# Transposes on two row tiles, PSUM as four fixed pairs, and a new order of the slot in a fused RWKV-7 and SoLU kernel

## The chip, the cores and the metric

The kernel runs on one core of one Trainium2 chip. A core has TensorE (matmuls, and the loads of their weights), VectorE, ScalarE and GpSimd for elementwise work, and SyncE, which here only issues DMAs. Every engine works through a queue of its own in order. Matmuls write PSUM, eight banks of 128 partitions by 512 float32; VectorE and ScalarE read it, GpSimd does not. The metric is the device time of one execution in microseconds.

## What is computed

Two blocks follow each other. The first is a recurrence over 768 tokens for 4 batches x 8 heads, each with a 40 x 40 state; the second takes its output, rearranged to 3072 tokens x 320, through a feed-forward layer with a softmax-weighted hidden layer and a normalisation.

```python
for t in range(S):                                   # batch 4, heads 8, S 768, D 40
    y[:, :, t] = einsum('bhd,bhde->bhe', rt, state)
    Sa = einsum('bhde,bhe->bhd', state, at)
    state = state * wt[:, :, None, :] - einsum('bhd,bhe->bhde', Sa, bt) + einsum('bhd,bhe->bhde', vt, kt)
x = y.transpose(0, 2, 1, 3).reshape(B * S, H * D)    # 3072 x 320
h = x @ w_in                                         # 3072 x 1024
solu = h * softmax(h)
ln = (solu - mean(solu)) / sqrt(var(solu) + 1e-6) * g_ln
out = ln @ w_out                                     # 3072 x 320
```

The weights of the second block are float64 and come in as their bits.

## The kernel before

**Tiling.** The recurrence is cut into chunks of 64 tokens. Two batches are stacked in the 128 partitions, so that there are N = 24 units of work (12 chunks x 2 pairs of batches), numbered `i`. Inside a unit the recurrence becomes small matrix products per batch and head, of 64 x 64, 64 x 40 or 40 x 64. TensorE runs them in its 64x64 form: four tiles of the array, two in the rows and two in the columns, each with its own weights. The products that use all 128 partitions (h, po, pcum) use the whole array.

**Stages of a unit.** `decay` takes logarithms of w, sums them with a matmul (pcum) and exponentiates. `decay_turned`, `front`, `front_b`, `attend_kv`, `attend_r` and `stated` transpose data from token rows to feature rows: `turned` (L347) makes four TensorE transposes of 128 partitions x 104 columns into one bank, and ScalarE or VectorE copies the result out. `norm` (L394) multiplies two of them, masks the product (`masked`, on VectorE) and writes it to DRAM, from where `spread` gathers 32 x 32 blocks for two units at a time. `invert` (L423) inverts these on VectorE in thirty steps of two instructions (prod, uu); the result goes through DRAM to `bring`. `flip`, `couple` and `close` complete the 64 x 64 inverse (tu); `scores`, `carried`, `driven`, `solved`, `answered`, `read` and `leave` compute the output of the unit and its new state.

**The feed-forward stages** run one to three units later, on the 128 tokens of a unit. `hidden` makes h (128 x 1024, two banks) from three slices of x: two of 128 rows, and one of 64 rows (`kt` = 2) whose two halves sit on the two row tiles. `highest`, `exped`, `weighed` and `spreadof` take the maximum (VectorE), the exponential with its sum (ScalarE), the product (VectorE), and the mean and variance by `bn_stats` (VectorE), with the power -1/2 on GpSimd. `folded` transposes the product in eight pieces of 128 x 128 (plnT), `output` multiplies by w_out in eight matmuls (po), and ScalarE scales the result on the way out (osb).

**PSUM** is held in three pools: `banks`, two buffers of two banks for everything on 64x64 tiles; h, one buffer of two banks; and `bank`, two single banks in turn for transposes, pcum, plnT and po. A buffer is taken by whoever asks next in the program, and its first matmul waits until the reader of the previous user is done.

**Order.** The order on every engine is written out by hand, in the loop at L823: each turn, or step, works on `i` (recurrence), `i + 1` and `i + 2` (its inputs), `j = i + 5` (the front of a later unit) and `m - 1` to `m - 3` with m = i - 1 (feed-forward). The inversion is dealt out in small numbers of steps between the other VectorE work (`some`, `narrow`; the tuple `pieces`). The first five steps also convert the weights to float32.

```python
L833        solved(i)
L837            scores(i + 1)
L844            stated(i); front(j)
L846        hidden(m - 2, ((0, 1),)); front_b(j); decay_turned(j + 1); hidden(m - 2, ((1, 1),))
L865        decay(j + 2); output(m - 3, 0)
L871        couple(i + 1); norm(j); answered(i); output(m - 3, 1)
L883        close(i + 1); read(i, True); carried(i + 1); hidden(m - 1, ((2, 0), (2, 1)))
L891        read(i, False); driven(i + 1); leave(i); folded(m - 2)
L896        hidden(m - 1, ((0, 0),)); attend_kv(i + 2); hidden(m - 1, ((1, 0),)); attend_r(i + 2)
```

Of the kernel before, what the change touches and what calls it, by code (L numbers as in the profile page):

```python
# [17 lines left out]
P = 128  # L18
# [9 lines left out]
THIN = (5, 15)  # L28
# [23 lines left out]
def kernel(  # L52
# [34 lines left out]
    ps1 = ctx.enter_context(tc.tile_pool(name="ps1", bufs=2, space=PSUM))  # L87
    ps2 = ctx.enter_context(tc.tile_pool(name="ps2", bufs=1, space=PSUM))
    ps3 = ctx.enter_context(tc.tile_pool(name="ps3", bufs=2, space=PSUM))
# [15 lines left out]
    nc.vector.memset(mhalf, -0.5)  # L105
    top = const.tile([P, 2], FP32, name="top")
# [15 lines left out]
    for x in ex_t:  # L122
# [10 lines left out]
                          in_=c_("eye_hi").unsqueeze(1).to_broadcast([P, 8, Q]))  # L133
    w_in = const.tile([P, 2 * NK - 1, DFF // 2], FP32, name="w_in")
# [4 lines left out]
    def banks(name):  # L139
        return ps1.tile([P, 2, 512], FP32, tag="banks", name=name)  # L140

    def bank(name):
        return ps3.tile([P, 512], FP32, tag="bank", name=name)
# [76 lines left out]
    def turn_g():  # L220
        pg = bank("pg")
        nc.tensor.transpose(out=pg[:, 0:NF], in_=g_rows, identity=ident[0:NF, 0:NF])
        for x, y in zip(g_cols, (0, -20, -36)):
            nc.scalar.mul(out=x, in_=pg[:, 0:NF], mul=2.0 ** y)
# [6 lines left out]
    def mean_of(lo, hi, begun):  # L231
        t = bank("pmean")
        nc.tensor.matmul(t[:, 0:DM], lhsT=ident, rhs=begun, start=True, stop=False)
        mean_part(t, lo, hi, False)
        return mean_kept(t)
# [90 lines left out]
    def decay(i):  # L326
# [5 lines left out]
        t = (bank("pcum") if i > 5 else ps2.tile([P, DFF], FP32, tag="h", name="h"))[:, 0:DM]  # L332
# [14 lines left out]
    def turned(name, x):  # L347
        t = bank("p" + name)
        for j in range(4):
            nc.tensor.transpose(out=t[0:W2, j * P:(j + 1) * P],  # L350
                                in_=x[:, 2 * j:2 * j + 2].rearrange("p a b -> p (a b)")[:, 0:W2], identity=ident)
        return t[0:W2].rearrange("p (j b t) -> p b j t", j=4, b=2)
# [9 lines left out]
    def decay_turned(i):  # L362
        if not ok(i):
            return
        ex = st[i]["ex"] = ex_t[i % (AHEAD + 2)]
        nc.scalar.copy(out=ex[0:W2, :, :, 1:], in_=turned("ei", ei_t[0]))

    def front(i):
        if not ok(i):
            return  # L370
        d = st[i]
        t = turned("a", d["raw_a"])
        aT = d["aT"] = tokens("aT", AHEAD)
        nc.vector.tensor_tensor(out=aT[0:W2], in0=t, in1=d["ex"][0:W2, :, :, 0:C], op=ALU.mult)

    def front_b(i):
        if not ok(i):
            return
        d = st[i]
        d["bT"] = kept("bT", turned("b", d["kb"][:, H:]))  # L380
# [13 lines left out]
    def norm(i):  # L394
# [3 lines left out]
        t = banks("pnt")  # L398
# [5 lines left out]
        masked(nt, t[:, :, 0:256])  # L404
# [18 lines left out]
    def invert(n):  # L423
# [6 lines left out]
        nc.vector.tensor_scalar(out=u[0:C], in0=nb[0:C, 0::2], scalar1=-1.0, scalar2=None, op0=ALU.mult)  # L430
# [36 lines left out]
    def couple(i):  # L467
# [3 lines left out]
        t = banks("py")  # L471
# [8 lines left out]
    def close(i):  # L480
# [3 lines left out]
        t = banks("pz")  # L484
# [8 lines left out]
    def attend_kv(i):  # L493
# [3 lines left out]
        d["kT"] = kept("kT", turned("k", d["kb"]))  # L497
        d["vT"] = kept("vT", turned("v", v_t[0]))

    def attend_r(i):  # L500
        if not ok(i):
            return
        st[i]["rT"] = kept("rT", turned("r", r_t[0]), 2)

    def stated(i):
        if not ok(i):
            return
        d = st[i]
        bp, ci = where_(i)
        if ci:  # L510
            t = bank("pst")
            for x in range(4):
                nc.tensor.transpose(out=t[0:W2, x * P:(x + 1) * P],  # L513
                                    in_=st_t[bp][:, 2 * x:2 * x + 2].rearrange("p a b -> p (a b)")[:, 0:W2], identity=ident)
            d["s"] = two.tile([P, 4, P], FP32, tag="s", name="s", bufs=1)
            nc.scalar.copy(out=d["s"][0:W2], in_=t[0:W2].rearrange("p (x t) -> p x t", x=4))

    def scores(i):
# [3 lines left out]
        t = banks("ps")  # L522
# [13 lines left out]
    def carried(i):  # L536
# [5 lines left out]
        d["px"] = banks("px")  # L542
# [21 lines left out]
    def solved(i):  # L564
# [3 lines left out]
        t = banks("pu")  # L568
# [14 lines left out]
    def answered(i):  # L583
# [3 lines left out]
        t = banks("pl")  # L587
# [6 lines left out]
    def read(i, own):  # L594
# [4 lines left out]
        if own:  # L599
            d["po"] = banks("pyo")  # L600
# [8 lines left out]
        for g in range(2):  # L609
            for j in range(2):  # L610
# [50 lines left out]
    def hidden(i, some):  # L661
# [4 lines left out]
        for kt, x in some:  # L666
            if (kt, x) == (NK - 1, 0):
                d["h"] = ps2.tile([P, DFF], FP32, tag="h", name="h")
            part = slice(0, P) if kt < 2 else half(x)
            mm(d["h"][:, 512 * x:512 * x + 512], d["xT"][part, kt], w_in[part, 2 * kt + (x if kt < 2 else 0)],  # L670
               start=kt == NK - 1, stop=kt == NK - 2)
# [16 lines left out]
    def weighed(i):  # L688
        if not ok(i):
            return  # L690
        d = st[i]
        nc.vector.tensor_tensor(out=d["e"], in0=d["h"], in1=d["e"], op=ALU.mult)  # L692

    def spreadof(i):
        if not ok(i):
            return
        d = st[i]
        bs = small.tile([P, 2, 6], FP32, tag="bs", name="bs")
        for x in range(2):
            nc.vector.bn_stats(out=bs[:, x], in_=d["e"][:, x * 512:x * 512 + 512])  # L700
        mv = small.tile([P, 2], FP32, tag="mv", name="mv")
        nc.vector.bn_aggr(out=mv, in_=bs)
        c = small.tile([P, 1], FP32, tag="c", name="c")
        c2 = small.tile([P, 1], FP32, tag="c2", name="c2")
        rs = d["rs"] = small.tile([P, 1], FP32, tag="rs", name="rs")
        nc.vector.tensor_scalar(out=c, in0=d["esum"], scalar1=1e-9, scalar2=None, op0=ALU.add)
        nc.vector.scalar_tensor_tensor(out=c2, in0=c, scalar=1e-6, in1=c, op0=ALU.mult, op1=ALU.mult)
# [224 lines left out]
```

## Time and profile before

| | |
|---|---|
| timed runs | 618.14, 618.70, 620.32 us (median 618.7) |
| the profiled execution, first to last instruction (span) | 616.2 us |
| TensorE, matmuls / weight loads | busy 552.0 us (90%) / 401.9 us (65%) |
| VectorE, ScalarE, GpSimd | busy 449.0, 265.8, 258.0 us (73%, 43%, 42%) |
| first pu of unit 4 / of unit 19 / of unit 23 | 161.4 / 485.3 / 561.7 us |
| mean clock granted to TensorE | 0.93; 0.52 to 0.64 from 19 to 115 us, 1.00 from 137 to 562 us |

The page gives no other time of its own for the profiled execution than its span. In its lines, PE is a matmul, PEld a weight load, DVE VectorE, ACT ScalarE and POOL GpSimd. A row of the windows gives the stretch, its length, then for each engine its busy time and its instructions, the granted clock, and the DMA engines' share and rate. A row of the timeline gives start, duration from the first start to the last end, engine, line, operation, the tile names, rows x columns of the stationary operand, partitions x columns of the output, and how many instructions; matmuls overlap, so the time that one group takes from the next is read from start to start. A float32 matmul is two instructions, a transpose one.

### The profile page before, as it was taken

What the parts mean: (1) busy time and instruction counts of PE and PEld (TensorE: products, weight loads), DVE (VectorE), ACT (ScalarE), POOL (GpSimd) and SP (SyncE); (2) the same over time, 40 slices, a digit from 0 to 9 for tenths busy, and PEclk for the clock granted to TensorE, in tenths of its full rate; (3) what the DMA queues carried; (4) which work ended last, traced back from release to release, by engine and by line L of the source; (5) the groups of instructions that cost most, each with busy time, mean ns of one, the idle gap of its engine ahead of it and who ended that gap; (6) DMA issues with size and microseconds to landing.
All of it is one profiled execution on the core that took longest, in us unless ns stands there. A gap on an engine that the chain in (4) does not pass through costs nothing.

```text
span 616.2 us, 26656 instructions
## 1 busy us (share of the span) xinstructions
PE 552.0 (90%) x11453; PEld 401.9 (65%) x11453; DVE 449.0 (73%) x1262; ACT 265.8 (43%) x548; POOL 258.0 (42%) x424
## 2 busy tenths in 40 slices
PE   5555668889999999999999999999999999999994
PEld 3333457666676777777777777777777676676652
DVE  4797986988968869869868868788697588443431
ACT  3433444654543544454444445444433343342221
POOL 3463264283453472473365355444624631322200
PEclk9665765789999999999999999999999999999998
DMA  7986887476455455564564474564532622310100
GB/s 164 159 156 121 183 157 129 98 156 104 76 106 104 90 115 99 93 122 95 100 123 91 95 126 98 112 113 82 110 56 53 118 49 43 65 35 26 28 19 21
DMA packets 213901, 59.93 MB, mean 97 GB/s; under 512 B 199120, under 2 KB 208952, under 8 KB 213784
## 3 DMA queue, kind: packets, MB, share of 16 engines
q1 hardware_dynamic: 195512, 33.78, 32.8%
q0 software_dynamic: 11568, 19.78, 14.0%
q10 hardware_dynamic: 6704, 4.67, 2.7%
q8 instruction: 90, 1.47, 1.0%
q14 instruction: 27, 0.22, 0.1%
HBM read 40.10 MB, written 13.37 MB: 87 GB/s over the span
## 4 chain that ended last, share of the span: by engine, by line
PE 74%; DVE 17%; ACT 3%; issue 3%; DMA 1%; ACTq 1%; DVEq 0%; SPq 0%
PE po L731 16%; PE h L265 16%; PE pyo L265 8%; DVE uu L438 5%; DVE prod L436 5%; PE pu L265 4%; PE plnT L720 4%; PE ps L265 4%; PE px L265 3%; PE py L265 2%; PE pl L265 2%; PE pz L265 2%; PE pr L350 2%; PE pst L513 2%; PE pcum L333 1%
## 5 line engine op out<-in xcount | busy, mean ns | idle before, releaser
L265 PE MATMUL h<-w_in,xT 128*128 128x512 f32 (+1 forms) x288 | 123.7, 614 | 0.0
L731 PE MATMUL po<-w,lnT 128*128 128x320 f32 x384 | 112.7, 438 | 0.5 <-ACT lnT L721 0.5
L438 DVE TENSOR_TENSOR uu<-uu,prod 128x30 f32<-128x30 f32 (+4 forms) x360 | 102.1, 284 | 12.4
L436 DVE TENSOR_TENSOR prod<-blk,uu 128x30 f32<-128x30 f32 (+4 forms) x360 | 99.2, 276 | 9.6
L731 PEld LDWEIGHTS po<-w,lnT 128*128 128x128 f32 x384 | 71.0, 190 | 32.6 <-issue 4.1
L409 POOL DMA_DIRECT2D nt_dram<-nt x20 | 18.8, 938 | 120.8 <-DVE nt L383 99.8
L709 POOL TENSOR_TENSOR rs<-c,mhalf 128x1 f32<-128x1 f32 x24 | 13.5, 561 | 112.3 <-DVE c L708 103.4
L383 DVE TENSOR_TENSOR psi<-ps,cst 128x512 f32<-128x512 f32 x24 | 16.6, 690 | 59.5 <-PE ps L265 59.5
L658 POOL DMA_DIRECT2D xT<-x x96 | 48.9, 514 | 0.4 <-DMA blk<-nt_dram 0.3
L265 PEld LDWEIGHTS h<-w_in,xT 128*128 128x128 f32 (+1 forms) x288 | 37.6, 190 | 9.4 <-issue 8.1
L678 DVE TENSOR_REDUCE nmax<-h 128x1 f32<-128x1024 f32 x24 | 28.6, 1193 | 18.6 <-PE h L265 18.6
L420 POOL DMA_DIRECT2D blk<-nt_dram x46 | 36.9, 808 | 11.8 <-issue 8.4
L265 PE MATMUL pyo<-lv,kb 64*64 64x104 f32 x768 | 38.3, 269 | 2.2
L265 PEld LDWEIGHTS pyo<-lv,kb 64*64 64x64 f32 x768 | 24.1, 142 | 21.2 <-issue 21.1
L265 PE MATMUL pyo<-lu,kb 64*64 64x104 f32 x768 | 37.4, 262 | 0.1
L646 POOL TENSOR_TENSOR st<-tot,ex 104x160 f32<-104x160 f32 x44 | 21.7, 511 | 36.4 <-DVE tot L642 32.4
L562 ACT COPY x<-px 128x320 f32<-128x320 f32 x24 | 10.2, 426 | 56.3 <-PE px L265 56.1
L477 ACT ACTIVATE wy<-py,cst 128x256 f32<-128x256 f32 x24 | 11.4, 474 | 53.2 <-PE py L265 53.2
L288 POOL DMA_DIRECT2D raw_r<-in_r_dram x48 | 33.9, 709 | 0.0
L735 ACT ACTIVATE osb<-po,rs 128x320 f32<-128x320 f32 x24 | 12.7, 527 | 48.5 <-PE po L731 32.8
L686 ACT ACTIVATE e<-h,nmax 128x1024 f32<-128x1024 f32 x24 | 26.6, 1108 | 14.3 <-DVE nmax L678 14.3
L692 DVE TENSOR_TENSOR e<-h,e 128x1024 f32<-128x1024 f32 x24 | 29.2, 1217 | 4.7 <-ACT e L686 4.7
(131 smaller groups left out, 1169.1 us busy)
## 6 DMA issues: line engine op xcount, KB each, us to landing
blk<-nt_dram POOLq DMA_DIRECT2D x46, 128.0 KB, 4.7
nt_dram<-nt POOLq DMA_DIRECT2D x20, 256.0 KB, 3.7
raw_w<-in_w_dram SPq DMA_DIRECT2D x48, 80.0 KB
a<-in_a_dram SPq DMA_DIRECT2D x48, 80.0 KB
raw_r<-in_r_dram POOLq DMA_DIRECT2D x48, 80.0 KB, 3.6
lv<-in_v_dram SPq DMA_DIRECT2D x48, 80.0 KB
out_dram<-osb ACTq DMA_DIRECT2D x24, 160.0 KB
raw_b<-in_b_dram SPq DMA_DIRECT2D x44, 80.0 KB
```

The lines of the kernel that those rows point to most:

```text
L265: nc.tensor.matmul(o, lhsT=lhsT, rhs=rhs, start=start, stop=stop, skip_group_check=True)
L288: queue.dma_start(out=x[half(p), :, 0:D], in_=ap[2 * bp + p, :, ci * C:(ci + 1) * C, :].rearrange("h t d -> t h d"))
L420: queue.dma_start(out=nb[home:home + Q], in_=blocks[n][:, Q * e:Q * e + Q, Q * e:Q * e + Q])
L436: nc.vector.tensor_tensor(out=t, in0=nb[:, j:j + 1, j + 1:Q].to_broadcast([P, n_c, m]), in1=u[:, 0:n_c, j:j + 1].to_broadcast([P, n_c, m]) ...
L438: nc.vector.tensor_tensor(out=u[:, 0:n_c, j + 1:Q], in0=u[:, 0:n_c, j + 1:Q], in1=t, op=ALU.subtract)
L646: nc.gpsimd.tensor_tensor(out=to3(old), in0=to3(tot[0:W2]), in1=ex[:, :, 2 * q:2 * q + 2, C:].to_broadcast([W2, 2, 2, D]), op=ALU.mult)
L658: nc.gpsimd.dma_start(out=xT[to:to + Q, 2], in_=x[at + P - 3 * D:at + D, 2])
L678: nc.vector.tensor_reduce(out=nmax, in_=d["h"], axis=AX.X, op=ALU.max, negate=True)
L686: nc.scalar.activation(out=e, in_=d["h"], func=AF.Exp, bias=d["nmax"], accum_out=d["esum"])
L692: nc.vector.tensor_tensor(out=d["e"], in0=d["h"], in1=d["e"], op=ALU.mult)
L720: nc.tensor.transpose(out=t[:, j * P:(j + 1) * P], in_=d["e"][:, f * P:(f + 1) * P], identity=ident)
L731: nc.tensor.matmul(d["out"][:, 0:DM], lhsT=d["lnT"][:, f, :], rhs=w2[:, f, :], start=f == 0, stop=f == NF - 1)
```

## The change

- `turned` and `folded` transpose in 64-row tiles. Where one transpose took 128 partitions and streamed the 128 columns of the identity, two now take 64 partitions each, stream 64 columns, and write two different banks. `stated` uses `turned` too.
- PSUM becomes four fixed pairs of banks, A, B, C and h, one buffer each. Every product names its pair. Two transposed tensors share a pair: state and a in C, b and ei in A, k and v in B; they are written first and copied out afterwards. The pair h also serves `couple` and `attend_r`.
- The step is put in another order, in eight runs of one form of the array: whole-array matmuls of h; pu, ps (64x64); the transposes pst, pa, pb, pei and the 64-row slice of h; h, pcum, h; pnt, pl, px, pyo (64x64); all eight matmuls of po; py, pyo, px, pz (64x64); pr, plnT, k, v (transposes). `hidden` starts with slice 0 in place of slice 2. `flip` stands behind `weighed` on VectorE, `logged` at the start of a step, and the inversion steps are dealt (5, 2, 2, 5) and (6, 2, 2, 6).
- The variance moves to ScalarE: the product sums itself up (mu), and Square with an accumulator, written over h, gives the sum of squares.
- `norm` stores its product unmasked, copied by ScalarE; `invert` masks the part that it needs with a constant, `above`, which GpSimd fills at the start.

```diff
-    ps1 = ctx.enter_context(tc.tile_pool(name="ps1", bufs=2, space=PSUM))
-    ps2 = ctx.enter_context(tc.tile_pool(name="ps2", bufs=1, space=PSUM))
-    ps3 = ctx.enter_context(tc.tile_pool(name="ps3", bufs=2, space=PSUM))
+    psum = ctx.enter_context(tc.tile_pool(name="psum", bufs=1, space=PSUM))
...
+    above = const.tile([C, Q // 2, Q], FP32, name="above")
+    nc.gpsimd.memset(above, 0.0)
+    for x in range(Q // 2):
+        nc.gpsimd.memset(above[:, x, 2 * x + 1:], -1.0)
...
+    def pair(tag, name):
+        return psum.tile([P, 2, 512], FP32, tag=tag, name=name)
+    def h_pair(name):
+        return psum.tile([P, DFF], FP32, tag="h", name=name)
...
-    def turned(name, x):
-        t = bank("p" + name)
+    def turned(t, y, x):
+        at = 256 * y
         for j in range(4):
-            nc.tensor.transpose(out=t[0:W2, j * P:(j + 1) * P],
-                                in_=x[:, 2 * j:2 * j + 2].rearrange("p a b -> p (a b)")[:, 0:W2], identity=ident)
+            for p in range(2):
+                nc.tensor.transpose(out=t[0:W2, p, at + C * j:at + C * j + C],
+                                    in_=x[half(p), 2 * j:2 * j + 2].rearrange("p a b -> p (a b)")[:, 0:W2],
+                                    identity=ident[half(p), half(p)])
...
-        masked(nt, t[:, :, 0:256])
+        nc.scalar.copy(out=nt, in_=t[:, :, 0:256].rearrange("p b (j c) -> p b j c", j=4))
...
-        nc.vector.tensor_scalar(out=u[0:C], in0=nb[0:C, 0::2], scalar1=-1.0, scalar2=None, op0=ALU.mult)
+        nc.vector.tensor_tensor(out=u[0:C], in0=nb[0:C, 0::2], in1=above, op=ALU.mult)
...
-        nc.vector.tensor_tensor(out=d["e"], in0=d["h"], in1=d["e"], op=ALU.mult)
+        nc.vector.scalar_tensor_tensor(out=d["e"], in0=d["h"], scalar=1.0 / DFF, in1=d["e"], op0=ALU.mult, op1=ALU.mult,
+                                       accum_out=d["mu"])
...
-        for x in range(2):
-            nc.vector.bn_stats(out=bs[:, x], in_=d["e"][:, x * 512:x * 512 + 512])
-        nc.vector.bn_aggr(out=mv, in_=bs)
-        nc.vector.tensor_scalar(out=c, in0=d["esum"], scalar1=1e-9, scalar2=None, op0=ALU.add)
-        nc.vector.scalar_tensor_tensor(out=c2, in0=c, scalar=1e-6, in1=c, op0=ALU.mult, op1=ALU.mult)
-        nc.vector.tensor_tensor(out=c2, in0=c2, in1=mv[:, 1:2], op=ALU.add)
-        nc.gpsimd.tensor_tensor(out=rs, in0=c2, in1=mhalf, op=ALU.pow)
+        nc.scalar.activation(out=c2, in_=d["esum"], func=AF.Square, scale=1e-3 / DFF, bias=guard)
+        nc.scalar.activation(out=d["h"], in_=d["e"], func=AF.Square, scale=-float(DFF), bias=d["mu"], accum_out=sq)
+        nc.scalar.activation(out=var, in_=sq, func=AF.Identity, scale=1.0 / DFF ** 3, bias=c2)
+        nc.gpsimd.tensor_tensor(out=rs, in0=var, in1=mhalf, op=ALU.pow)
...
+        t = pair("C", "plnT")
+        for f in range(NF):
+            for p in range(2):
+                nc.tensor.transpose(out=t[:, p, f * C:f * C + C], in_=d["e"][half(p), f * P:(f + 1) * P],
+                                    identity=ident[half(p), half(p)])
...
+        solved(i); scores(i + 1)
+        t = pair("C", "pst")
+        for evict in [stated(i, t, 0), front(j, t, 1)]: evict()
+        t = pair("A", "pb")
+        for evict in [front_b(j, t, 0), decay_turned(j + 1, t, 1)]: evict()
+        hidden(m - 2, ((2, 0), (2, 1))); hidden(m - 2, ((0, 1),)); decay(j + 2); hidden(m - 2, ((1, 1),))
+        highest(m - 2); scaled(j + 1); left(i - 1); norm(j); exped(m - 2); by_value(i + 2)
+        answered(i); carried(i + 1); weighed(m - 2); read(i, True); spreadof(m - 2)
+        output(m - 3); flip(i + 1); fence(); couple(i + 1, "h"); read(i, False); driven(i + 1)
+        close(i + 1); leave(i); attend_r(i + 2, "h"); folded(m - 2); attend_kv(i + 2)
+        hidden(m - 1, ((0, 0), (1, 0)))
```

The other products take these pairs: pnt, pu, pyo A; ps, pcum, pl, po, pz B; px C. In the last lines the calls of the new loop stand in their order, several to a line, without the conditions and the inversion steps between them.

## The prediction

> **What bounds the kernel now.** I read four views in this order: the page, busy time by step, one step of the middle instruction by instruction, and the groups of weight loads.
>
> ```profile
> PE 552.0 (90%) x11453; PEld 401.9 (65%) x11453; DVE 449.0 (73%) x1262; ACT 265.8 (43%) x548; POOL 258.0 (42%) x424
> PEclk9665765789999999999999999999999999999998
> PE 74%; DVE 17%; ACT 3%; issue 3%; DMA 1%; ACTq 1%; DVEq 0%; SPq 0%
> ...
> 115.00:137.40 22.40, 17.11 (x396) 12.35 (x388) 20.32 (x57) 13.33 (x28) 13.51 (x22) 0.92 0.72 142
> 292.20:313.70 21.50, 21.31 (x486) 15.70 (x489) 15.87 (x47) 10.06 (x21) 11.16 (x20) 1.00 0.57 111
> ```
>
> The chain that ended last is 74% TensorE. The two window rows show why an average misleads. Up to about 161 us VectorE is the busiest engine (20.32 of 22.40) and the clock is granted in part; from there to 485 us every step is 20.7 to 22.5 us long and TensorE is busy for all but 0.2 to 0.4 of it, at clock 1.00. There, a step is the sum of what TensorE streams. VectorE (15.87) and ScalarE (10.06) have room.
>
> ```profile
> 289.84 0.60 PE L350 MATMUL pk<-cst,kb 128*104 128x128 f32 x4
> 290.28 0.60 PE L350 MATMUL pv<-cst,v 128*104 128x128 f32 x4
> ...
> 300.44 0.67 PE L265 MATMUL py<-tu,nt 64*64 64x32 f32 x32
> 300.93 0.67 PE L265 MATMUL pnt<-aT,bT 40*64 40x64 f32 x32
> 301.71 0.69 PE L265 MATMUL pl<-rT,nuT 40*64 40x64 f32 x32
> ...
> 307.03 1.13 PE L265 MATMUL h<-w_in,xT 64*128 64x512 f32 x4
> 308.25 0.41 PE L265 MATMUL pyo<-lv,kb 64*64 64x104 f32 x8
> ...
> 309.57 1.10 PE L720 MATMUL plnT<-cst,e 128*128 128x128 f32 x8
> 310.50 1.02 PE L265 MATMUL h<-w_in,xT 128*128 128x512 f32 x2
> ```
>
> Take start to start. Four full transposes cost 0.43 to 0.44 us, 107 ns each; the eight of plnT cost 0.93. With pr (0.53) and pst (0.48) the seven groups and plnT make 4.12 of the 21.52 us from one pu (292.11) to the next (313.63). py, 32 instructions on four 64x64 tiles, costs 0.49: 15.3 ns each, 61 ns per turn of a tile. pnt costs 0.78 instead of 0.49, because pl behind it needs the PSUM buffer that py left and ScalarE must empty it: 0.78 us from the end of py's stream to pl, 0.29 of it uncovered. The four two-row-tile matmuls of h cost 1.22, where four in sequence would be 4 x 0.43 = 1.72: two row tiles do stream at once.
>
> **The price that decides: one transpose in a 64-row tile.** It streams 64 columns in place of 128, so 53 ns by the rate above, on two tiles at once. But there are twice as many weight loads, and each still loads 104 columns (128 for plnT). Is a turn of a tile set by the stream or by the load?
>
> ```profile
> L731 PEld LDWEIGHTS po<-w,lnT 128*128 128x128 f32 x384 | 71.0, 190 | 32.6 <-issue 4.1 <-ACT ex L366 2.1 <-ACT lnT L721 0.8
> L720 PEld LDWEIGHTS plnT<-cst,e 128*128 128x128 f32 x192 | 20.6, 141 | 3.7 <-issue 1.8 <-PE po L731 0.7
> L265 PEld LDWEIGHTS pz<-uh,wy 64*64 64x64 f32 x768 | 14.6, 145 | 12.9 <-issue 7.0 <-DVE nt L383 5.0 <-DVE lu L383 0.9
> ...
> 571.46 0.30 PEld L265 LDWEIGHTS h<-w_in,xT 64*128 64x128 f32 x4
> 574.38 0.30 PEld L265 LDWEIGHTS h<-w_in,xT 128*128 128x128 f32 x2
> ```
>
> The fourth number of a group row is the mean of one in ns. A 128-column load of an ordinary matmul takes 190 ns, a 64-column one 145, and a 128-column load of a transpose only 141: a transpose loads 128 columns in the time of 64 ordinary ones. Two full loads take 0.30 us and one 0.19, so an ordinary load occupies 0.11 per 128 columns; four half-height loads also take 0.30, so loads of two row tiles run together. By the row that it is nearest to (the transposes' own 141) the load occupies some 55 ns, beside 53 of stream, and I take 57 ns a turn, between 53 and the 61 of a 64x64 turn. A group of eight is four turns: 0.23 us for 0.43. plnT is eight turns: 0.46 for 0.86. The other ends: 0.21 if only the stream counts; and, if the load goes at the ordinary 0.11 per 128 columns, 0.36 a group and 0.88 for plnT.
>
> [...]
>
> **The change, part by part, for a middle step.**
> - Transposes. 7 x 0.43 + 0.86 = 3.87 us becomes 7 x 0.23 + 0.46 = 2.07: -1.8.
> - Order by tile form. Both orders change the form eight times a step at about 0.1 each (pr, ahead of a 64x64 run, takes 0.53 where pk and pv take 0.43), so this is worth nothing by itself. The two-row-tile matmuls of h join the run of transposes of the same form: 1.22 to about 0.96, -0.25. The uncovered wait at pnt (0.29) and 0.11 in the second half of po go, since po now lies between pl's eviction and py. TensorE's sum: 21.52 - 1.8 - 0.65 = 19.1.
> - Four fixed pairs. Each PSUM use now waits for the eviction of the one before it in its pair. Laid out by hand from rows, with 0 where h's last matmul ends: nmax 0.2 to 1.4, exp to 2.7, lu on VectorE to 2.1, two inversion steps (0.6 each) to 3.3, the product to 4.6, Square on ScalarE to 5.9, var to 6.1. TensorE meanwhile runs pnt, pl, px, pyo and all eight of po until 7.2, so py finds pair h free. ScalarE then does osb to 7.9, issues the output (0.52) to 8.4, and wy to 8.9; px ends at 8.9, so pz starts with nothing to spare. x0 is out at 9.5, tu at 10.0, rT at 10.5; plnT is needed from 9.7, pkv from 10.2, h from 10.65. All covered, by 0 to 0.3 us; pyo behind nt likewise. I add 0.3 for waits that show (bounds 0 and 3.9, see the rivals): 19.4 a step, -2.1.
> - Variance. VectorE loses two statistics (0.69 each), the aggregate (0.21) and three small ones (0.10, 0.16, 0.16), and the masking of nt (0.69): -2.7. The product may gain an accumulator read, 0 to 0.2 (ScalarE's is 0.20). It then holds 13.4 to 15.5 of 19.4. ScalarE gains nt (0.59), Square with its read (1.11 + 0.20, as Exp) and two one-column activations (0.18 each, as g's): 12.3 of 19.4. GpSimd's pow waits for var instead of c. Behind it queue the state update and the loads of raw_r; the update needs tot, later than var, so the wait costs nothing.
> - above. 17 memsets on GpSimd (0.53 + 16 x 0.12 = 2.5 us) lie in the 5.3 us in which it waits for the first inv. Each inversion starts with a two-operand product instead of a scaling: 0.68 for 0.42, once in two steps, on VectorE; in the middle that is idle time.
> - aT waits for s, both reading pair C: s is out about 1.05 us after ps ends, VectorE comes to aT at 1.4. Nothing.
>
> **The sum.** The page's span is 616.2; the timed runs are 618.1 to 620.3, so about 2.5 us lie around the span and I carry the difference to the median of 618.7.
> - 15 steps, 161 to 485 us: 15 x 2.1 = -32.
> - Three steps without the front of new chunks (485 to 544): four groups and plnT, 4 x 0.2 + 0.4, and 0.4 of waits: 3 x 1.6 = -5.
> - Two more (to 574): -1.
> - Up to 161 us VectorE carries it: eight maskings (8 x 0.69) and one variance (1.9) out, four products (4 x 0.26) in, -6.4 on an engine busy for 130.6 of 161.4: I take -5. Bounds: -11, and +5 if the single buffers stall the few matmuls there.
> - Tail: h is held until Square ends, 5.6 us after its last matmul, against po and plnT of 4.9: +0.1 for each of three steps; at the end lnT waits on ScalarE behind Square, var, osb and a DMA issue: +1.3. Together +1.6.
> - Sum -41.4: 577 us.
>
> **The rivals.**
> - *The loads set the turn.* Groups 0.36, plnT 0.88: 21.52 - 0.65 + 0.3 - 3.87 + 3.40 = 20.7, -0.8 a step. 12 + 5 + 2 - 1.6 = 17 less: 601. For it: the 0.11 of the ordinary loads; against: 141 beside 190.
> - *Row tiles that do not overlap on transposes,* so that the change does not do what it says: 3.87 stays, -0.3 a step, 610. Against it: the 1.22 of h.
> - *ScalarE becomes the bound through its order; slower.* Square waits for the product, and behind it in the queue stand osb, wy, x0, tu, rT, each of which frees a pair. If it runs late, five places pay a full turn-around like py's 0.78: 3.9 a step, 19.1 + 3.9 = 23.0, +1.5 x 18 - 5 + 2: 643. It decides from 2.4 us of waits a step on. For it: cover of 0 to 0.3 us; against: ScalarE is 63% busy, and lateness at one place gives cover to the next.
>
> **How the numbers follow.** The forecast 0.55, the loads 0.24, no overlap 0.07, ScalarE 0.14. With the prologue's bounds, the stream's end (0.21) and no waits at all, the first runs from 563 to 587; the second, with the prologue's bounds, from 595 to 611. Leaving out ScalarE's case and the extremes gives 562 to 608. Under 0.3% (1.9 us) this kernel cannot be told from no change. The third and fourth case at their mild ends give 0.03 for that; faster 0.85, slower 0.12.
>
> **What would show it.** Groups pa, pb, pk at 0.23 per eight and plnT at 0.46, start to start; a middle step of 19.4; po in one run of eight; no bn statistics; no wait of TensorE over 0.3 us in the middle. Wrong if the transposes stay at 0.36 or more, or if pz, pkv or h wait for ScalarE by more than 2 us a step, or if the first 161 us grow.

## The result, and the profile after

The changed kernel takes **623.12 us** (median of 20 runs, 619.37 to 631.44) beside 618.84 (614.66 to 623.64) for the kernel before on the same chip: a ratio of 1.0061, 95% interval 1.0037 to 1.0086. It is slower by 0.6%; the forecast was 577. The ratio leaves out two slow runs of the changed kernel, 630.67 and 631.44 us, that the medians include. Its profiled execution took 621.36 us, its span is 619.5.

From the page of the changed kernel (busy times; granted clock in 40 slices; the queue that brings instructions: packets, MB, share of the DMA engines; the chain that ended last):

```profile
PE 518.1 (84%) x12309; PEld 367.3 (59%) x12309; DVE 404.5 (65%) x1119; ACT 317.3 (51%) x668; POOL 261.6 (42%) x441
...
PEclk9655656599999999999899989999999999999999
...
q8 instruction: 97, 1.59, 1.1%
...
PE 63%; DVE 17%; issue 8%; DMA 5%; ACT 3%; POOL 1%; SPq 0%; ACTq 0%; DVEq 0%; POOLq 0%
```

TensorE's work fell from 552.0 to 518.1 us, and VectorE's from 449.0 to 404.5. But TensorE's share of the chain fell from 74% to 63%, and "issue", time in which an engine waits for nothing that the profile shows, rose from 3% to 8%. The clock, at 9 tenths or more of full speed in every slice from 139 us on before but the last, now has two slices at 8. The instruction queue moved 97 packets instead of 90.

The timeline of TensorE in the changed kernel (start, duration, group, count; in brackets the idle time in front and what ended it):

```profile
302.81 0.56 PE L268 MATMUL pz<-uh,wy 64*64 64x32 f32 x22
305.89 0.63 PE L268 MATMUL pz<-uh,wy 64*64 64x32 f32 x10 [2.52 <-issue]
306.45 0.67 PE L355 MATMUL pr<-cst,r 64*104 64x64 f32 x8
306.92 1.06 PE L731 MATMUL plnT<-cst,e 64*128 64x64 f32 x16
307.77 0.63 PE L355 MATMUL pkv<-cst,kb 64*104 64x64 f32 x8
...
360.98 0.70 PE L268 MATMUL pu<-tu,x 64*64 64x64 f32 x32
...
363.00 0.43 PE L355 MATMUL pst<-cst,st 64*104 64x64 f32 x8
363.27 0.39 PE L355 MATMUL pst<-cst,a 64*104 64x64 f32 x8
363.50 0.39 PE L355 MATMUL pb<-cst,kb 64*104 64x64 f32 x8
363.72 0.39 PE L355 MATMUL pb<-cst,ei 64*104 64x64 f32 x8
...
377.18 0.43 PE L355 MATMUL pr<-cst,r 64*104 64x64 f32 x8
377.45 0.66 PE L731 MATMUL plnT<-cst,e 64*128 64x64 f32 x16
377.95 0.39 PE L355 MATMUL pkv<-cst,kb 64*104 64x64 f32 x8
...
380.40 0.69 PE L268 MATMUL pu<-tu,x 64*64 64x64 f32 x32
```

The lower part is a step without a stop: from pu at 360.98 to pu at 380.40 it takes 19.42 us, the forecast to the hundredth, but by luck: the other step of the fifteen that has no stop takes 20.27, and the mean, given below, is 19.8. Its groups of eight transposes take 0.22 to 0.27 from start to start and plnT 0.50. The upper part is what the forecast lacks. After 22 of the 32 matmuls of pz TensorE stands still for 2.52 us in the middle of a run, waiting for nothing that the profile shows, and what follows takes 1.7 times as long (pr 0.47 instead of 0.27, plnT 0.85 instead of 0.50). The windows of the changed kernel around it, and TensorE's waits in the middle (total, times, longest):

```profile
303.00:306.00 3.00, 0.48 (x29) 0.36 (x25) 1.53 (x6) 0.43 (x1) 2.22 (x4) 0.99 0.86 151
306.00:309.00 3.00, 3.00 (x51) 2.80 (x52) 2.20 (x5) 1.94 (x5) 2.98 (x5) 0.50 0.50 130
```

```profile
PE px L268 <- issue: 4.5, 4, 3.6
PE pkv L355 <- issue: 4.1, 4, 2.1
PE pz L268 <- issue: 3.8, 2, 2.5
PE pst L355 <- issue: 3.1, 3, 1.5
PE pb L355 <- issue: 2.4, 2, 1.4
```

After the stop the granted clock is 0.50 in this window. The list above has the changed kernel's five largest entries; the whole list has no wait for ScalarE. The kernel before has one entry in its middle:

```profile
PE ps L265 <- issue: 0.2, 1, 0.2
```

Summed over the 15 middle steps (pu of unit 4 to pu of unit 19), stops that end 1.15 to 1.7 us after a packet of the instruction queue has landed make 24.4 us, and 10.2 us at half clock cost 5.1 more (time lost to the half clock is given so from here on); the kernel before has 0.2 and 0. Without the two a step takes (326.6 - 29.5) / 15 = 19.8 us, before 21.6. So the change won 27 us in the middle, and stops and half clock took 29.5.

### The profile page after: what moved, and what is told of

The parts are those of the page before. It is cut to its first block, busy times and chain, and to the rows that moved or that the text cites. A ratio compares the mean times of both kernels' runs of the same rounds, so it can differ in the third digit from the quotient of the medians.

```text
span 619.5 us, 28385 instructions
## 1 busy us (share of the span) xinstructions
PE 518.1 (84%) x12309; PEld 367.3 (59%) x12309; DVE 404.5 (65%) x1119; ACT 317.3 (51%) x668; POOL 261.6 (42%) x441
## 3 DMA queue, kind: packets, MB, share of 16 engines
q8 instruction: 97, 1.59, 1.1%
## 4 chain that ended last, share of the span: by engine, by line
PE 63%; DVE 17%; issue 8%; DMA 5%; ACT 3%; POOL 1%; SPq 0%; ACTq 0%; DVEq 0%; POOLq 0%
PE h L268 18%; PE po L745 12%; DVE uu L450 5%; PE pyo L268 5%; DVE prod L448 5%; PE pu L268 4%; PE ps L268 4%; PE px L268 3%; PE py L268 2%; PE plnT L731 2%; PE pst L355 2%; PE pcum L336 2%; PE pkv L355 2%; PE pz L268 2%; DMA blk<-nt_dram 2%
## 5 line engine op out<-in xcount | busy, mean ns | idle before, releaser
L448 DVE TENSOR_TENSOR prod<-blk,uu 128x30 f32<-128x30 f32 (+4 forms) x360 | 104.7, 291 | 29.7 <-DMA blk<-nt_dram 19.0
L745 PE MATMUL po<-w,lnT 128*128 128x320 f32 x384 | 109.5, 438 | 1.8 <-ACT lnT L735 1.8
L268 PEld LDWEIGHTS h<-w_in,xT 128*128 128x128 f32 (+1 forms) x288 | 41.0, 191 | 43.0 <-issue 38.4
L721 POOL TENSOR_TENSOR rs<-var,mhalf 128x1 f32<-128x1 f32 x24 | 13.5, 564 | 100.5 <-ACT var L720 99.9
L639 DVE TENSOR_TENSOR x<-pyo,ex 104x256 f32<-104x256 f32 x48 | 18.1, 419 | 46.6 <-PE pyo L268 43.9
L336 PE MATMUL pcum<-lw,cst 128*128 128x320 f32 x48 | 23.5, 579 | 22.4 <-ACT lw L327 21.5
L719 ACT ACTIVATE h<-e,mu 128x1024 f32<-128x1024 f32 x24 | 26.8, 1118 | 19.8 <-DVE e L706 19.8
L268 PE MATMUL pyo<-lu,kb 64*64 64x104 f32 x768 | 29.4, 262 | 5.4 <-DVE lu L395 3.1
L706 DVE SCALAR_TENSOR_TENSOR e<-h,e 128x1024 f32<-128x1024 f32 x24 | 29.3, 1219 | 5.8 <-ACT e L698 5.8
L268 PE MATMUL py<-tu,nt 64*64 64x32 f32 x768 | 17.7, 230 | 17.3 <-DVE tu L477 11.3
```

Of the source, the lines that this page charges most:

```text
L268: nc.tensor.matmul(o, lhsT=lhsT, rhs=rhs, start=start, stop=stop, skip_group_check=True)
L336: nc.tensor.matmul(t, lhsT=c_("cum"), rhs=d["lw"], start=True, stop=True)
L448: nc.vector.tensor_tensor(out=t, in0=nb[:, j:j + 1, j + 1:Q].to_broadcast([P, n_c, m]), in1=u[:, 0:n_c, j:j + 1].to_broadcast([P, n_c, m]) ...
L706: nc.vector.scalar_tensor_tensor(out=d["e"], in0=d["h"], scalar=1.0 / DFF, in1=d["e"], op0=ALU.mult, op1=ALU.mult, accum_out=d["mu"])
L719: nc.scalar.activation(out=d["h"], in_=d["e"], func=AF.Square, scale=-float(DFF), bias=d["mu"], accum_out=sq)
L745: nc.tensor.matmul(t, lhsT=d["lnT"][:, f, :], rhs=w2[:, f, :], start=f == 0, stop=f == NF - 1)
```

## The experiments

**Theory F:** TensorE's instructions arrive in blocks of 256 (16 KB; one pair of load and matmul is two), and it stops when it has used up a block before the next is there. 1.59 MB over 97 packets is 16 KB each, and 24618 loads and matmuls over 97 are 254. The new order puts the 64x64 runs and the now shorter transposes together, so that some blocks last under 3 us. **Rival S:** the stops belong to the groups in which they fall, to their PSUM pairs or their forms.

**1. The same stream, shifted by half a block.**

```diff
+    idle = pair("A", "idle")
+    for _ in range(32):
+        mm(idle[0:C, 0, 0:Q], ident[0:C, 0:C], ident[0:C, 0:Q])
```

> The changed kernel with 64 matmuls with loads (32 small float32 products into a bank that is overwritten later) ahead of everything on TensorE: half a block of instructions. Theory F: the stops move by 64 matmuls back through the step. Where the changed kernel stops in pst, pb or k behind pu and ps (183.7, 220.3, 241.6 us), those steps stop elsewhere, at places half a block away, such as pr, px or pyo; their number stays near 26; the time stays within 612 to 632. Theory S, or a DMA that comes late: the stops stay at the same instructions, time 623 to 625.

Measured: 629.87 us, ratio 1.0201 (1.0144 to 1.0258). The number of stops stays (23 of over 0.25 us from 140 us on, 29.2 us; 24 and 26.8 in the changed kernel), their places move: pz, which had two in the middle, now has seven of over 1.1 us, and pst none. S falls. What settles it is a count. TensorE's instructions numbered in the built program (loads, matmuls, and waits that are instructions of their own), the first matmul after each stop of over 0.3 us stands at these places modulo 256:

```
changed kernel        23 stops from 140 us on: 194 or 195, all
shifted by 64 pairs   23 stops: 22 at 194 or 195
full transposes       11 stops: 10 at 194 or 195
```

(The third row is experiment 2.) By the profile the two that stand elsewhere are waits for other engines: pyo for VectorE's lu, pz for ScalarE's wy.

**2. The transposes alone taken back** (order, pairs and variance as in the changed kernel).

```diff
-        for j in range(4):
-            for p in range(2):
-                nc.tensor.transpose(out=t[0:W2, p, at + C * j:at + C * j + C], ...
+        for j in range(4):
+            nc.tensor.transpose(out=t[0:W2, y, j * P:(j + 1) * P], ...
```

> The changed kernel with the transposes alone undone: full transposes of 128 rows, four for eight and eight for sixteen, each group in one bank of its pair. Theory F: the stream grows by 1.8 us a step (7 x 0.21 + 0.36), but 36 matmuls with their loads fall away and the runs of short instructions last longer, so that most of the 1.3 us of stops per step and the slow clock behind the long ones go: 21.2 + 0.4 = 21.6 a step, 614 to 624 us, the same as the changed kernel. Theory S: evictions and order are the same, so the waits stay and the stream comes on top: 18 x 1.8 = 32 us more, about 655.

Measured: 634.85 us, 1.0286 (1.0245 to 1.0327); above F's range, below S's 655. A step without a stop takes 21.24 us, as worked out, beside 19.42; by the means net of stops and half clock it is 21.29 beside 19.81. So two row tiles are worth 1.5 to 1.8 us a step. But 12.3 us of stops remain in the middle, with 5.1 for half clock: the order by itself, with 64x64 runs side by side, makes blocks too short, which F's range had not allowed for, and the short transposes double the stops.

**3. The same instructions, long matmuls spread among the short ones.**

```diff
+        hidden(m - 2, ((1, 0),))       # between pu and ps
...
-        output(m - 3)
+        output(m - 3, 0, 6)            # the other two after px
...
-        hidden(m - 1, ((0, 0), (1, 0)))
+        hidden(m - 1, ((0, 0),))       # ahead of attend_kv
...
```

> The changed kernel, but with TensorE's long matmuls spread among its short ones: po as 6 + 2 matmuls, the last two between px and pr; h slice 0 between pz and k, h slice 1 between pu and ps, the last matmul of h between pnt and pl. Same instructions, same tiles. Theory F (instruction fetch): TensorE's instructions arrive in blocks of 16 KB (97 packets on the instruction queue, 1.59 MB), some 127 matmuls with their loads; the trace of the changed kernel shows it stopping in the middle of a run of short matmuls wherever a block was used up in under about 3.5 us, and going on 1.3 to 1.6 us after the next packet has arrived. Spread out, hardly a block is used up that fast: a step of 19.4 us without stops, plus seven more changes of form at 0.1, plus 0.3 of stops left, is 20.4 for the 21.8 measured; 15 steps and three shorter ones give about 598 us (590 to 608). Theory S (ScalarE and the single-buffered pairs): osb, rT and tu now come closer together and the waits stay or grow: 620 us or more.

Measured: 626.5 us, 1.0153 (1.0113 to 1.0193). This misses F's 590 to 608 and is what S forecast (620 or more), but not by S's way: stops fall to 5.4 us in the 15 steps and no half clock is left, as F has it. A step without a stop now takes 21.2 us instead of 19.4 (21.27 and 19.81 by the means net of stops and half clock). Seven changes of form more and a wait for rT (3.9 us in 15 steps) make these 1.5 to 1.8 us: about 0.2 a change, where I had priced 0.1.

**4. The kernel before with a dense run added:** the first product of pu is made three times.

```diff
-        for u in in_turn(lambda p, q, g, h: (p ^ h, q)):
+        for _ in range(3):
+            for u in in_turn(lambda p, q, g, h: (p ^ h, q)):
...
```

> The kernel before with the first product of pu made three times (64 more short matmuls with loads in one row, 192 short ones in all between two long ones); the result is the same. The stream grows by 1.0 us in each of 24 steps, twice that in the five at half clock: about +28. Theory F: a block now often lies wholly inside the 192, which last 3.0 us, so the order of the kernel before begins to stop as well, about 1 us a step: 655 to 670 us, with stops in pu, ps or the transposes behind them. Without F: 643 to 649 and no stops.

Measured: 661.66 us, 1.0728 (1.0681 to 1.0774). The old kernel, given one dense place, shows the same thing there: 12 stops marked "issue" of over 0.25 us from 140 us on (13.1 us), nearly all in ps, pu and pa behind pu, and half clock three times. F holds; nothing of the change is needed for it.

**5. The price by itself:** chains without any wait.

> Left out: the whole computation; the output is zeros. TensorE alone runs chains that wait for nothing. Chains of 384 pairs of load and matmul on four 64x64 tiles, with 32, 104, 128 and 160 columns each, first with no data moving (quiet), then beside loads of 1 MB that follow each other (busy); and groups of one, two or four 128x512 matmuls in turn with four, eight or sixteen 64x64 matmuls, the same work with half and a quarter of the changes of form. Theory F (instructions arrive in blocks of 256, and TensorE stops where it has used up a block in under about 3.5 us): at the 15.3 ns a pair of py a block lasts 1.94 us, at the 22.8 of pyo 2.9, and at 128 and 160 columns some 3.6 and 4.5. So the quiet chain of 32 columns takes about 10 us in place of 5.9 and shows stops of about 1.5 us every 126 pairs, that of 104 about 10 in place of 8.8, those of 128 and 160 show none. In the busy chains stops of 2 us or more, and some at 104 and 128 columns. Rival S (the stops come from what the groups of the changed kernel do, not from the rate of instructions): no chain stops; 5.9, 8.8, 11 and 14 us. Cost of a change of form: 32 groups against 16 pairs of groups have 32 changes more: 3.2 us more at the 0.1 that the prediction took, 6.4 at the 0.2 that the run with spread matmuls gave.

The timeline of TensorE in this run (the start of each pattern is enough for the changes of form: "full" are 1, 2 or 4 matmuls of two instructions each, in turn with 8, 16 or 32 short instructions):

```profile
40.59 1.13 PE L104 MATMUL full<-mov,cst 128*128 128x512 f32 x2
...
82.32 1.98 PE L104 MATMUL full<-mov,cst 128*128 128x512 f32 x4
...
118.79 3.70 PE L104 MATMUL full<-mov,cst 128*128 128x512 f32 x8
...
152.62 1.13 PE L104 MATMUL fullt<-mov,cst 128*128 128x512 f32 x2
...
204.09 3.92 PE L104 MATMUL quiet<-mov,cst 64*64 64x32 f32 x251
208.83 2.06 PE L104 MATMUL quiet<-mov,cst 64*64 64x32 f32 x128 [0.82 <-issue]
212.28 0.31 PE L104 MATMUL quiet<-mov,cst 64*64 64x32 f32 x5 [1.39 <-issue]
...
223.00 8.57 PE L104 MATMUL quiet<-mov,cst 64*64 64x104 f32 x359
231.94 0.83 PE L104 MATMUL quiet<-mov,cst 64*64 64x104 f32 x25 [0.37 <-issue]
...
241.49 10.71 PE L104 MATMUL quiet<-mov,cst 64*64 64x128 f32 x384
...
300.38 4.03 PE L104 MATMUL busy<-mov,cst 64*64 64x32 f32 x259
307.81 2.71 PE L104 MATMUL busy<-mov,cst 64*64 64x32 f32 x125 [3.39 <-issue]
```

Stops 128 pairs apart: F. At 32 columns 128 pairs stream in about 2.0 us, and from stop to stop it takes 3.45 (208.83 to 212.28); at 104 columns the last block takes 3.45 too; at 128 columns a block streams in 3.49 and nothing stops. So a block in these quiet chains costs 3.45 us or its stream, whichever is longer. The stops were fewer than expected (8.3 us for the chain of 32 columns, not 10), because a second block was already there when the chain began: the edge at 205.9 us passes without a stop, and the last packet ahead of it had landed at 197.4. Beside loads of 1 MB (DMA engines fully busy, 418 GB/s) a stop is 3.39 us, and a block of 104 columns pays 2.15. Behind the stop of 1.39 us the clock was at half for 3.4 us, behind that of 3.39 us, with one of 0.63 in it, for 10.2.

The changes of form: the same work takes 41.73 us with 64 changes, 36.47 with 32, 33.83 with 16. (41.73 - 36.47) / 32 = 0.164 and (36.47 - 33.83) / 16 = 0.165 us a change, between the 0.1 taken and the 0.2 above.

**6. One h matmul moved between pu and ps.**

```diff
         solved(i)
+        hidden(m - 2, ((1, 0),))
...
-        hidden(m - 1, ((0, 0), (1, 0)))
+        hidden(m - 1, ((0, 0),))
```

> The changed kernel with one move: of the two h matmuls ahead of pu one stays, the other goes between pu and ps. Two changes of form more, at 0.2 each: a step without a stop takes 19.8 us. Theory F: the dense stretch from py to the last transpose is now broken by 0.95 us twice; if a block may not be used up in under 3.5 us, the stops fall from 1.2 to 0.8 us a step in the model, by a third, and the half clock behind long stops mostly goes: 26.8 us of stops become about 18, 5 us of half clock about 2, the extra changes cost 7: 614 to 623. Rival S (stops belong to the groups in which they fell): 26.8 us stay, and the changes come on top: 630.

Measured: 617.88 us, 0.9999 (0.9965 to 1.0034). Stops in the middle 17.0 us for 24.4, a step without them 20.04 for 19.81. Half clock stayed at 5.1, where F had 2. Time and stops are as F had them; a cheap repair that wins back what the change had lost.

**7. The variance alone taken back to VectorE.**

> The changed kernel with the variance back on VectorE as before, so that ScalarE loses Square (1.3 us) and h is free earlier. Theory F: in the middle neither engine sets the step; a step without a stop stays 19.4, the stops stay at some 24 to 32 us, and only the tail gets shorter by about 1.5 us: 619 to 624. Rival (ScalarE became the bound through its order): the small waits behind it go and the middle gets shorter by 10 us or more: 613 or less.

Measured: 616.78 us, 0.9969 (0.9934 to 1.0004); below F's range, above the rival's. A step without stops is the same (19.85 and 19.81), so neither engine sets it, and the time from the last po to the end is 0.7 us shorter. The 15 steps are 11.0 us shorter, as the rival had it, but not for its reason: stops are 16.1 us for 24.4 and half clock 1.7 for 5.1, in a stream of which each step has one instruction fewer. I take it for another fall of the block edges, and the next runs test how much that can be.

**8. The block edges held in place.** With full transposes for pr and plnT alone, a middle step has 506 pairs, with its waits 1023 or 1024 instructions: four blocks, so that the edges stand at the same places in every step. Idle pairs ahead of the kernel move all of them.

```diff
-        st[i]["rT"] = kept("rT", turned(pair(tag, "pr"), 0, r_t[0]), 2)
+        for j in range(4):
+            nc.tensor.transpose(out=t[0:W2, j * P:(j + 1) * P], ...
...
+    idle = pair("A", "idle")
+    for _ in range(73):                # in the second kernel only
+        nc.tensor.transpose(out=idle[0:C, 0, 0:C], in_=ident[0:C, 0:C], identity=ident[0:C, 0:C])
```

> The changed kernel with full-array transposes for pr and plnT alone (12 pairs of load and matmul fewer in a step, and 0.7 us more in it by the rows: 0.43 + 0.93 for 0.27 + 0.50 and one or two changes of form). A middle step then has 506 pairs, with its waits 1023 to 1024 instructions of TensorE, four blocks of 256, so that the edges of blocks stand at the same places of every step: in the program, 59 to 62 pairs behind the start of pu, then in pnt, pyo and px. Theory F: the stops so far all stand at one place of the count of 256, so now every step has the same stops at these places. By the rule that a block may not be used up in under 3.5 us, with the durations of a step of the changed kernel that has no stop, this is nearly the worst place: 1.6 us of stops a step, 24 in 15 steps, and as the rule gave 18 where 24 were measured, 24 to 32; half clock costs 5 to 10 more. A step without a stop would be 20.5, one with them 22 to 23: 635 to 650. Rival S (edges of blocks don't matter): 0.7 a step more than the changed kernel, 634, with the stops where they were.

> The same kernel with 73 idle pairs of load and matmul ahead of everything, at the start, where TensorE is not what is waited for. The edges of blocks then stand 114 to 117 pairs behind the start of pu, in px, in py and at the end of pkv, in all middle steps; every block then holds long matmuls and lasts 4.0 us or more. Theory F: no stops and no half clock from 161 to 486 us; a step 20.3 to 20.5; 15 steps 19 us less than in the changed kernel (326.6 in its profile), some 2 more behind them: 600 to 610, 30 us or more under the run without the idle pairs, from which it differs by nothing else. Rival S: the same time as that run, or 3 us more.

Measured: without idle pairs 628.04 us, 1.0137 (1.0086 to 1.0188); with 73 idle pairs 613.65 us, **0.9923** (0.9889 to 0.9957). TensorE's waits between 160 and 492 us, and the window (its row ends with granted clock, DMA share and rate), without idle pairs and with them:

```profile
PE px L268 <- issue: 9.5, 5, 3.1
PE pz L268 <- issue: 5.3, 2, 2.9
...
PE pyo L268 <- issue: 0.5, 1, 0.5
```

```profile
160.00:492.00 332.00, 310.83 (x7577) 225.81 (x7578) 233.18 (x656) 182.09 (x384) 161.96 (x260) 0.97 0.50 100
```

```profile
PE pkv L355 <- issue: 3.5, 6, 1.0
PE py L268 <- issue: 1.6, 7, 0.3
```

```profile
160.00:492.00 332.00, 320.83 (x8029) 231.85 (x8027) 247.36 (x692) 190.41 (x402) 165.72 (x266) 1.00 0.51 102
```

Two programs that differ by 73 idle pairs at the start differ by 14 us: 17.1 us of stops and 10.2 of half clock in 15 steps against 5.7 and none. (The two profiled executions are 18 us apart; that with idle pairs is the fastest of its eight.) In the same 332 us the second gets through 452 more matmuls. All stops of the first are in px, pz and pyo or in pu, where the count puts the edges. The size was off both ways: the second is 4 us above its range, and the first is better than its 635 to 650, and not stopped where the rule said. The rule's 1.6 us a step belong at pyo, the one edge behind a block of under 3.5 us (it streams in 2.0 to 2.3); pyo stopped in two steps (0.67 and 0.54 us). Nine of the eleven stops, 15.9 of the 17.1 us, end blocks that stream for 5.7 to 7.3 us. Seven of the nine, at px or pz, end the block right behind the short one: there the fetch of the next block began 6.3 to 7.9 us after the block was entered. So the place of the edges is shown to be worth the 14 us, but 3.5 us a block is not a full account of the stops.

**9. The held edges and the variance on VectorE,** with 73 and with 80 idle pairs.

> The run with 73 idle pairs, with the variance back on VectorE. Its steps have one instruction fewer, the edges drift from 114 to 124 pairs behind pu, still a good place. Theory F with ScalarE off the path: the middle as in the run with 73 idle pairs, the tail 1 us shorter: 0 to 2 us less than that run. Rival (variance on ScalarE costs 5 us, as the run with it alone taken back would say if its stops were no accident): 5 us less or more than that.

> The run with 73 idle pairs and the variance on VectorE, with 80 idle pairs, so that the drift of the edges lies in the middle of the good place: 107 to 117 pairs behind pu in the middle steps instead of 114 to 124. Theory F: no stop above 0.6 us and no half clock from 161 to 486 us; 606 to 612, and as a whole under both kernels. Rival S: as the run with 628, or more.

Measured: 611.9 us, 0.9876 (0.9814 to 0.9938), and 612.13 us, **0.991** (0.9881 to 0.994). Once the edges are held, the variance is worth no more than the runs' intervals leave open (613.65 beside 612); the 6 us of experiment 7 lie by its profile in the stops. With 80 idle pairs stops fall to 3.7 us in the 15 steps, the longest 0.72, with no half clock; F had 0.6 and at most 612. Both are faster than the kernel before and than the changed one.

**10. The norm masked on VectorE again,** with 73 idle pairs.

```diff
-        nc.scalar.copy(out=nt, in_=t[:, :, 0:256].rearrange(...))
+        masked(nt, t[:, :, 0:256])
```

> The run with 73 idle pairs, with the norm masked on VectorE as before (and the two-operand product in front of an inversion a scaling again, without the table for it). For the prediction's term on the first 161 us, where VectorE was to win 5 us and the profile of the changed kernel shows 1. Theory 1 (VectorE's work is what those 161 us are made of; the other 4 went to something else in the change): taking the maskings back costs them their price, 8 x 0.69 less 4 x 0.26, 4 to 5 us, all ahead of 161 us: 617 to 619. Theory 2 (VectorE spends there what it wins on waiting for ScalarE, which has taken the norm over, so that the two cancel): within 1.5 us of the run with 73 idle pairs. In the middle neither expects a difference, as VectorE is busy for 0.7 of it.

Measured: 620.86 us, 1.0041 (1.0012 to 1.007): 7 us more, and neither theory had it. The first part is as long as before (pu of unit 4 at 162.5, without the masking at 161.9), which is theory 2's half, though from one profile of each. The middle grew from 312.2 to 319.8 us:

```profile
PE pyo L264 <- DVE nt L391: 6.4, 15, 1.1
```

In all 15 steps TensorE now waits for VectorE ahead of pyo, mostly 0.38 us. pnt and pyo use the same pair of banks, A, and pyo starts 0.06 us after VectorE has masked nt out of it, each time. VectorE comes to nt only behind nmax (at 321.73 us, when pnt had started at 320.48) and takes 0.68; in the run without the masking ScalarE copied nt out from 0.76 us behind the start of pnt, in 0.58. VectorE is busy for 0.7 of the middle, and yet 0.69 us at this place cost 0.5 a step.

## Why the prediction was wrong

- **Transposes on two row tiles:** right. Groups 0.22 to 0.27, plnT 0.50 with a change of form, forecast 0.23 and 0.46. The rivals "loads set the turn" and "no overlap" fall.
- **TensorE's sum of a step, 19.4:** near. The best step takes 19.42, the mean net of stops and half clock is 19.8; the 0.4 between I have not followed. The waits in it are as forecast: 3.9 us in 15 steps (0.26 each, I had 0.3), mostly at py.
- **"There, a step is the sum of what TensorE streams":** the step that failed. I carried it from a trace in which it was true to an order in which it isn't, and worked out "All covered, by 0 to 0.3 us" for waits between engines alone. Missing was the supply of instructions: 24.4 us of stops and 5.1 of half clock in the 15 steps, against 26.8 won. Of the 23 stops 13 (14.5 us) end a block that streamed in 2.2 to 3.0 us; the other ten (9.9 us) end blocks of 4.1 to 7.2 us in which the fetch of the next began only 1.9 to 8.4 us after the entry. The trace of before held one sign, a stop at ps, 1.3 us behind an instruction packet and at the same place of the count of 256, inside the "issue 3%" that I quoted and did not follow:

```profile
487.83 0.58 PE L265 MATMUL ps<-rT,vT 40*64 40x64 f32 x24 [0.89 <-issue]
```

- **"Order by tile form ... is worth nothing by itself":** wrong. Its eight changes cost 0.165 instead of 0.1, which cancels between the two orders; but the order puts py, pyo, px and pz, then pr to pkv, and pu to ei side by side, 328 pairs with one run of long matmuls (1.9 us of h) among them. With full transposes it has 12.3 us of stops where the old order has 0.2.
- **The first 161 us, -5:** measured -1.0. VectorE's busy time there fell by 4.5 us, but its waits grew: those for ScalarE (ex, and the scales of the weights) from 7.5 to 16.0 and those for DMAs from 0 to 5.3, while those for TensorE fell from 14.2 to 3.9. In experiment 10 the masking is worth 0.6 us there, in one profile of each; runs with nearly the same first part differ by 3 us there (157.1 in experiment 6, 160.3 in the changed kernel), so the cause stays open.
- **485 to 544 us, -5:** measured -2.0, with 2.1 us of stops in it.
- **From 544 us on, -1 and +1.6:** the tail is right in its parts. An iteration at the end takes 10.13 us for 9.98, and the last po waits 1.78 us for lnT instead of 0.53 (the two lines below). But from 544 us to the end the kernel lost 3.6 where the two terms make 0.6; a stop at 546.7 us is 0.7 of it, and some 2 I have not followed.

The changed kernel:

```profile
607.42 4.57 PE L745 MATMUL po<-w,lnT 128*128 128x320 f32 x16 [1.78 <-ACT lnT L735]
```

The kernel before:

```profile
604.21 4.57 PE L731 MATMUL po<-w,lnT 128*128 128x320 f32 x16 [0.53 <-ACT lnT L721]
```

- **The rival that ended slower** had the right side and the wrong mechanism: ScalarE, at 317.3 us, makes TensorE wait nowhere in the middle: its waits there are marked "issue" or VectorE.
- The terms add up: -1.0 + 2.7 (323.9 to 326.6) - 2.0 + 3.6 = +3.3, the difference of the spans.

## What to carry to other kernels

Where a step is made of many short matmuls, count instructions as well as time. In these runs 256 of them in a row that streamed in 2.0 to 3.0 us often left TensorE waiting for the next ones, at their end or a block later (0.3 to 3.65 us in the changed kernel), at times with half clock behind it; in the quiet chains 3.49 us a block went without a stop. Making the short ones shorter, or sorting them together to save changes of form (0.165 us each), moved against that. What paid it back was a long matmul in between (experiment 6, 617.88 us beside the changed kernel's 623.12), or a step whose instructions are a multiple of 256 with the edges placed in long runs (experiment 8, 613.65 beside 628.04). And "issue" in a profile is a row to be followed like any other.

## What the runs showed of the hardware

- Instructions of TensorE come in blocks of 256: 55 of the 57 stops in the table of experiment 1, all but the two that wait for other engines, fall at one place of that count, 194 or 195. The price is 3.45 us a block in a quiet chain (stop at 212.28 us): the fetch starts 1.1 us after the block is entered, takes 1.0, and TensorE goes on 1.3 later.
- The fetch can start late. Ahead of the stop of 3.65 us in the changed kernel it began 8.4 us after the block was entered, and in the run of experiment 8 without idle pairs, up to 340 us, 6.3 to 7.9 us in the steps that stopped at px, against 0.7 to 1.1 in those that didn't. In the busy chains, with full DMA engines, it began 2.9 to 3.7 us after the entry. In the six steps of that run the DMA engines' share behind the entry was 0.66 to 0.75 where the fetch was late, and 0.24, 0.38 and 0.65 where it wasn't: that fits, and doesn't settle what delays it. One thing goes with it: in the 15 steps of the two kernels and of all the variants, 27 fetches began more than 4.5 us after the entry, and in 26 of them the block before had streamed in 3.0 us or less. The kernel before and the runs with 73 or 80 idle pairs, where all blocks but one stream for 3.3 us or more, have none.
- The clock halved at some stops: behind 1.39 us in the chain, 1.64 in experiment 6 and 2.52 in the changed kernel, and there in the last 0.5 us of a stop of 3.65. Others, of 1.75 and 2.12 us in the changed kernel (up to 263.24 and 484.71 us; granted clock 1.00 behind both), had no such sequel. In the traces of both kernels the stretches at half clock begin a multiple of 3.41 us apart (305.92 and 353.71 us in the changed kernel: 14 of them; 90.42 and 127.96 in the kernel before: 11); whether the place of a stop between such times decides is not shown.
